# Turning two batches' exponentials through DRAM instead of on TensorE, and moving a clamp from VectorE to ScalarE

## The chip, the cores and the metric

The kernel runs on one core of one Trainium2 chip. The metric is the device time of one launch in microseconds (us), the median of several runs. The engines are named as the profile names them: PE is TensorE (matrix products and transposes through the array), PEld its weight loads, DVE is VectorE, ACT is ScalarE, SP is the engine whose queue issues all DMAs here, POOL is GpSimd.

## The reference

Inputs are `x` (8 batches, 8 heads, 512 positions, 64), `state` (8, 8, 32, 64), `moe_w_in` (512 x 2048) and `moe_w_out` (2048 x 512); all are float32, and the two weights arrive as 64-bit floats (two 32-bit words each). Cut to what matters:

```python
scores  = x @ state.T / 8        # per batch and head: 512 x 32
xread   = softmax(scores) @ state
scores2 = state @ x.T / 8        # 32 x 512
e2      = exp(scores2 - scores2.max(-1))
sread   = (e2 / (e2.sum(-1) + 1e-9)) @ x          # 32 x 64
tokens  = concat([xread, sread], positions)       # (8*544) x 512
h       = tokens @ w_in                           # (8*544) x 2048
out     = (h * sigmoid(1.702*h)) @ w_out          # (8*544) x 512
```

## The kernel before

The order of the instructions on every engine is the order of the program; nothing is rescheduled. Three parts matter.

**The weights.** Each of 32 pieces (16 of w_in, then 16 of w_out: one piece is 128 rows x 512 columns) is loaded as pairs of words and put together as float32. VectorE takes the exponent bits (`mask`), they are clamped to the range of float32 and rescaled (`round_a`), and VectorE makes the number of fraction and exponent (`fraction`, `round_b`). For w_in ScalarE clamps, with two Relu passes; for w_out VectorE clamps, with two passes.

```python
def mask(i):
    _, hi = words(i)
    sc = low[:, 2 + i % (AHEAD + 1)].bitcast(I32)
    power[i] = sc
    nc.vector.tensor_scalar(sc, hi, 0x7FF00000, None, ALU.bitwise_and)        # L207

def round_a(i):
    if i not in power:
        mask(i)
    sc = power[i]
    if PIECES[i][0] == "o":
        nc.vector.tensor_scalar(sc, sc, most, least, ALU.min, ALU.max)        # L215
        nc.vector.tensor_scalar(sc, sc, -least, 8.0, ALU.add, ALU.mult)       # L216
        return
    nc.scalar.activation(out=sc.bitcast(FP32), in_=sc, func=AF.Relu, bias=edge[0], scale=-8.0)    # L218
    nc.scalar.activation(out=sc, in_=sc.bitcast(FP32), func=AF.Relu, bias=edge[1], scale=-1.0)    # L219

def round_b(i, ahead, follows):
    if i not in begun:
        fraction(i)                                                           # L225
    ...                    # dst: the piece's place; lo, hi: its words; sc: its exponent
    nc.vector.scalar_tensor_tensor(sc, hi, -0x80000000, sc, ALU.bitwise_and, ALU.bitwise_or)      # L236
    powers_to(ahead)       # mask and round_a of the pieces up to `ahead`
    nc.vector.scalar_tensor_tensor(dst, lo, 2.0**-32, dst.bitcast(I32), ALU.mult, ALU.add)        # L239
    if follows and i + 1 in raw:
        fraction(i + 1)
    nc.vector.scalar_tensor_tensor(dst, dst, 2.0**-20, sc.bitcast(FP32), ALU.mult, ALU.mult)      # L243

def round_to(n, ahead=AHEAD):
    ...
        powers_to(i + 1)
        round_b(i, min(i + 1 + ahead, max(nin, i + 1)), i + 1 < nin and (i + 1 < n or i >= NPR))
    # nin = 16: the number of w_in's pieces; afterwards the next loads are issued
```

The raw words of w_out's pieces share four places in the tile `later`: piece 4 of w_out can be loaded when piece 0's words have been read (L239), and so on.

**The exponentials.** `sread` multiplies e2, turned so that the 512 positions lie on partitions, with x. For batches 0 and 1 TensorE turned it, and VectorE had multiplied it by the inverse sums; batches 2 to 7 went by 32x32 blocks through DRAM and were scaled after the product.

```python
def s_norm(b, g):
    e, sm = A[b]["e2"][g]
    nc.vector.tensor_scalar(sm, sm, eps, None, ALU.add)
    nc.vector.reciprocal(out=sm, in_=sm)
    if b < 2:
        nc.vector.tensor_scalar(e, e, sm, None, ALU.mult)                     # L381

def eT_out(b):                       # batches 2 to 7; e in 32x32 blocks to DRAM
    for j in range(NPR):
        src = e2_room[b][Ns * j : Ns * (j + 1), :NG].rearrange("n g (t a) -> n (g t) a", a=Ns)
        nc.sync.dma_start(squares[:, :, j], src)                              # L468
def eT_in(b):                        # ... and back, the blocks in their turned places
    ...
    for i in range(SCH):
        nc.sync.dma_start(a["eT"][Ns * i : Ns * (i + 1)].rearrange("n g c q -> n (g c) q"), v[i])   # L476
def eT_turn(b, g):                   # ... and each block turned
    t = A[b]["eT"][:, g].rearrange("p c q -> p (c q)")
    nc.vector.transpose(t, t)                                                 # L480

def att_eT(b, g):                    # batches 0 and 1
    ...
    for c in range(SCH):
        nc.tensor.transpose(ps[:, c], a["e2"][g][0][:, P * c : P * (c + 1)], ident)   # L489
    nc.scalar.copy(a["eT"][:, g], ps)                                         # L490
```

**The loop over w_out's pieces.** It multiplies batch 0 (`down`) while batch 1's hidden rows are still being made (`up_x`, whose gelu is ScalarE's). One turn of it is called a stage.

```python
rounds(1)                            # w_out piece 0; piece 1 follows after four up_x of batch 0
...
rest = list(range(2 * nper, NF))     # the last 8 of the 16 up_x of batch 1
for f in range(NF):                  # NF = 16
    rounds(1)                        # finishes piece f + 2, while there is one
    ...
    if f == NF - 1:
        up_x(1, rest.pop(0))
    for r in range(SCH):
        down(0, r, [f], out_x[0, r], r == SCH - 1)        # 4 products, L542
    if f == 0:
        for b in range(2):
            for g in range(NG):
                att_eT(b, g)
    if f == 1:
        att_sread(0); att_sread(1)                        # L500, copied out by ScalarE
        att_M(1, 2, True); att_M(1, 3)                    # L320, copied out by ScalarE
    if f == 2:
        att_srT(0); att_srT(1)
    if f == 2 or f % 2 == 1 and 1 < f < NF - 1:
        up_x(1, rest.pop(0))                              # L524 on TensorE, gelu L527 on ScalarE
    if f == HF:
        load_state(2); load_x_squares(2)
    if f == NF - 2:
        T_of(T1, B12, B11)                                # L1203: sums of w_out for Strassen's products
        ...
# batch 1: strassen_two, whose products P1, P2 and then the low ones (L689) follow at once
```

Of the kernel before, what the change touches and what calls it, by code (L numbers as in the profile page):

```python
# [10 lines left out]
FP32 = mybir.dt.float32  # L11
I32 = mybir.dt.int32
U32 = mybir.dt.uint32
AF = mybir.ActivationFunctionType
ALU = mybir.AluOpType
# [5 lines left out]
def kernel(  # L21
# [30 lines left out]
    nc = tc.nc  # L52

    B, H, S, D = x.shape
    Ns = state.shape[2]
    DM = H * D
    DF = moe_w_in.shape[1]
    P = 128
    NPR = P // Ns
    NG = H // NPR  # L60
    NF = DF // P
    SCH = S // P
# [3 lines left out]
    NB = S // Ns  # L66
    HF, HN = NF // 2, DM // 2
    scale = float(1.0 / np.sqrt(D))
# [12 lines left out]
    apool = ctx.enter_context(tc.tile_pool(name="apool", bufs=1))  # L81
# [3 lines left out]
    dram = ctx.enter_context(tc.tile_pool(name="dram", bufs=1, space=bass.MemoryType.DRAM))  # L85
# [6 lines left out]
    def att_ps(shape, name):  # L92
        return psA.tile(shape, FP32, tag="att", name=name)

    ident = konst.tile([P, P], FP32, name="ident")
# [70 lines left out]
    PIECES = [("i", c, k) for c in range(NFC) for k in range(NPR)] + [("o", f) for f in range(NF)]  # L166
# [26 lines left out]
    for i, v in enumerate((8.0 * most, 8.0 * (most - least))):  # L193
        t = konst.tile([P, 1], FP32, name=f"edge_{i}")
# [7 lines left out]
# [9 lines that stand above are left out]
        if i not in power:  # L211
            mask(i)
        sc = power[i]
        if PIECES[i][0] == "o":
            nc.vector.tensor_scalar(sc, sc, most, least, ALU.min, ALU.max)  # L215
            nc.vector.tensor_scalar(sc, sc, -least, 8.0, ALU.add, ALU.mult)  # L216
            return
        nc.scalar.activation(out=sc.bitcast(FP32), in_=sc, func=AF.Relu, bias=edge[0], scale=-8.0)  # L218
        nc.scalar.activation(out=sc, in_=sc.bitcast(FP32), func=AF.Relu, bias=edge[1], scale=-1.0)  # L219

    def fraction(i):

        key = PIECES[i]
        dst = w_in[key[1]][:, key[2]] if key[0] == "i" else w_out[:, key[1]]
        nc.vector.tensor_scalar(dst.bitcast(I32), words(i)[1], 0xFFFFF, 0x100000, ALU.bitwise_and, ALU.bitwise_or)  # L225
        begun[i] = dst
# [6 lines that stand above are left out]
        dst = begun.pop(i)  # L233
        lo, hi = words(i)
        sc = power.pop(i)
        nc.vector.scalar_tensor_tensor(sc, hi, -0x80000000, sc, ALU.bitwise_and, ALU.bitwise_or)  # L236
        powers_to(ahead)

        nc.vector.scalar_tensor_tensor(dst, lo, 2.0**-32, dst.bitcast(I32), ALU.mult, ALU.add)  # L239
        del raw[i]  # L240
# [3 lines that stand above are left out]
# [19 lines left out]
    def round_to(n, ahead=AHEAD):  # L263

        nin = NFC * NPR
        while done["b"] < min(n, len(PIECES)):
            i = done["b"]
            powers_to(i + 1)
            round_b(i, min(i + 1 + ahead, max(nin, i + 1)), i + 1 < nin and (i + 1 < n or i >= NPR))
            done["b"] += 1  # L270
            while done["b"] > NPR and done["load"] < len(PIECES) and before(done["load"]) < done["b"]:
                load_weights(done["load"] + 1)
# [12 lines left out]
    A = {b: {} for b in range(B)}  # L285
# [76 lines left out]
    e2_room = {}  # L362

    def att_s_exp(b, room=None):
        a = A[b]
        if room is None:
            room = e2_room[b] = apool.tile([P, NPR, S], FP32, tag="xT", name=f"e2_{b}")
        a["e2"] = []
        for g in range(NG):
            e = room[:, g]  # L370
            sm = apool.tile([P, 1], FP32, tag="sm2", name=f"sm2_{b}_{g}", bufs=4)
            nc.scalar.activation(out=e, in_=a["s"][g], func=AF.Exp, bias=a["mx2"][g], scale=scale, accum_out=sm)
            a["e2"].append((e, sm))

    def s_norm(b, g):

        e, sm = A[b]["e2"][g]
        nc.vector.tensor_scalar(sm, sm, eps, None, ALU.add)
        nc.vector.reciprocal(out=sm, in_=sm)
        if b < 2:  # L380
            nc.vector.tensor_scalar(e, e, sm, None, ALU.mult)  # L381

    def att_s_norm(b):
        for g in range(NG):
# [75 lines left out]
            nc.scalar.copy(m[:, g], ps[g])  # L460


    squares = dram.tile([Ns, NG * NB, NPR, Ns], FP32, name="squares")

    def eT_out(b):
        for j in range(NPR):
            src = e2_room[b][Ns * j : Ns * (j + 1), :NG].rearrange("n g (t a) -> n (g t) a", a=Ns)
            nc.sync.dma_start(squares[:, :, j], src)  # L468

    def eT_in(b):  # L470

        a = A[b]
        a["eT"] = apool.tile([P, NG, SCH, P], FP32, tag="eT", name=f"eT_{b}")
        v = squares.rearrange("n (k i) j a -> i n k (j a)", i=SCH)
        for i in range(SCH):
            nc.sync.dma_start(a["eT"][Ns * i : Ns * (i + 1)].rearrange("n g c q -> n (g c) q"), v[i])  # L476

    def eT_turn(b, g):
        t = A[b]["eT"][:, g].rearrange("p c q -> p (c q)")
        nc.vector.transpose(t, t)  # L480

    def att_eT(b, g):

        a = A[b]
        if g == 0:
            a["eT"] = apool.tile([P, NG, SCH, P], FP32, tag="e1" if b else "eT", name=f"eT_{b}")
        ps = att_ps([P, SCH, P], f"eT_{b}_{g}")
        for c in range(SCH):
            nc.tensor.transpose(ps[:, c], a["e2"][g][0][:, P * c : P * (c + 1)], ident)  # L489
        nc.scalar.copy(a["eT"][:, g], ps)  # L490

    def att_sread(b):

        a = A[b]
        ps = att_ps([P, NG, D], f"sr_{b}")
# [3 lines that stand above are left out]
                    st = slice(Ns * j, Ns * (j + 1))  # L499
                    nc.tensor.matmul(  # L500
                        ps[st, g], a["eT"][:, g, c, st], xn[b][:, c, NG * j + g],
                        start=(c == 0), stop=(c == SCH - 1),
                    )
        sr = apool.tile([P, P], FP32, tag="sr", name=f"sr_{b}", bufs=2)
        if b < 2:
            nc.scalar.copy(sr, ps.rearrange("p g d -> p (g d)"))
        else:
            for g in range(NG):
                nc.scalar.activation(out=sr[:, D * g : D * (g + 1)], in_=ps[:, g], func=AF.Copy, scale=a["e2"][g][1])
        A[b]["sr"] = sr  # L510

    def att_srT(b):
# [607 lines left out]
    def rounds(n):  # L1120
        round_to(done["b"] + n)
# [64 lines left out]
    turn(0, 2, (0, 3))  # L1186
    room = apool.tile([P, NPR, S], FP32, tag="xT", name="e2_01")
    att_s_exp(0, room[:, :NG])
    att_s_exp(1, room[:, NG:])
    rounds(1)  # L1190
    att_s_norm(0)
    att_s_norm(1)
# [27 lines left out]
    for f in range(NF):  # L1220
        rounds(1)
        round_to(NFC * NPR + f + 1)
        if f == NF - 1:

            up_x(1, rest.pop(0))
        for r in range(SCH):
            down(0, r, [f], out_x[0, r], r == SCH - 1)
        if f == 0:
            for b in range(2):
                for g in range(NG):  # L1230
                    att_eT(b, g)
        if f == 1:

            att_sread(0)
            att_sread(1)
            att_M(1, 2, True)
            att_M(1, 3)
        if f == 2:
            att_srT(0)
            att_srT(1)  # L1240
        if f == 2 or f % 2 == 1 and 1 < f < NF - 1:
            up_x(1, rest.pop(0))
        if f == HF:
            load_state(2)
            load_x_squares(2)
        if f == NF - 2:
            T_of(T1, B12, B11)
            low_away(6, B22)
            low_made(5, T1, 1)
            for u in range(NU - 1):  # L1250
                s12(1, u, S)
            T_of(T2, B22, T1)
            low_third(T1)
            for u in range(NU - 1):
                s3(1, u, S)
            T_of(B12, B22, B12)
            low_away(3, T3)
            low_third(T3)
        if f == NF - 1:
            turn_x(2)  # L1260
            low_made(2, T2, 0)
# [6 lines left out]
    for b in range(1, B):  # L1268
        if b > 1:
            ahead = {"P1a": [(up_strassen(b, S, *parts_x(b), A[b]["sums"]), ())]}  # L1270
        else:
            ahead = {
                "P1a": [(low_third, (B22,)), (T_of, (T4, B21, T2)), (low_third, (T2,)), (low_away, (4, T4)), (low_third, (T4,))]
            }
# [19 lines left out]
        k = 3 if b + 1 < B else 0  # L1294
# [40 lines left out]
```

## Time and profile before

| what | before |
|---|---|
| time, median of 3 runs | 708.99 us (708.97 to 709.4) |
| span of the profiled run | 706.9 us |
| VectorE busy | 602.4 us (85%) |
| ScalarE busy | 230.8 us (33%) |
| L489, 16 transposes of e on TensorE | 2.2 us busy, 81.3 to 83.7 us |
| L215 and L216 | 0.43 us each |
| L218 and L219, the same clamp on ScalarE | 0.71 and 0.72 us each |
| L480, the turn of 128x512 on VectorE | 0.69 us each |

How to read the profile: its page gives the busy time of each engine, the chain of work that ended last (followed back from the last instruction, at each step to what released it), and groups of instructions by line of the kernel, with tile names `out<-in`. A view in order of time has a start, a length, the engine, the line, and in brackets the idle time before it and what ended that. [...] neighbours overlap: the difference of two starts is what an instruction costs in a full row. One 128x512 product is listed as two instructions (x2).

### The profile page before, as it was taken

Reading aid. Unit: us, or ns where it says so; the run is one execution under the profiler, and the core shown is the slowest. Engines: PE = TensorE matmul, PEld = TensorE weight load, DVE = VectorE, ACT = ScalarE, POOL = GpSimd, SP = SyncE. Lnnn points to the kernel's source line nnn. Section 1 sums busy time; section 2 is a strip of 40 time slices with the busy share of each in tenths; the row PEclk is TensorE's granted clock in tenths of the full one; section 3 lists DMA queues with packets and bytes.
Section 4 is the critical chain, followed back from the end, with each engine's and each line's share of the span. In section 5 each row is a group of like instructions: output and inputs, shape, how many; then the busy total and the mean of one; then the engine's idle time right before and its main releaser. Section 6 shows DMA issues by size and latency. Waiting matters only on the chain.

```text
span 706.9 us, 12667 instructions
## 1 busy us (share of the span) xinstructions
PE 694.9 (98%) x4973; PEld 558.1 (79%) x4975; DVE 602.4 (85%) x1246; ACT 230.8 (33%) x456; POOL 0.8 (0%) x8
## 2 busy tenths in 40 slices
PE   8989999999999999999999999999999999999996
PEld 3433544458998799879988899889987998899995
DVE  6999799999978998799978996899789987888650
ACT  5686520014224413433243423342243124200210
POOL 0000000000000000000000000000000000000000
PEclk9999999999999999999999999999999999999999
DMA  8921246228742384309550765047432940041001
GB/s 230 368 74 54 93 146 154 115 89 206 213 118 37 61 194 145 69 9 206 148 105 1 152 182 120 16 82 199 137 51 48 194 148 16 0 125 57 16 1 29
DMA packets 143914, 77.89 MB, mean 110 GB/s; under 512 B 113904, under 2 KB 127728, under 8 KB 143856
## 3 DMA queue, kind: packets, MB, share of 16 engines
q1 hardware_dynamic: 143856, 77.09, 42.3%
q8 instruction: 39, 0.64, 0.4%
q14 instruction: 19, 0.16, 0.1%
HBM read 61.08 MB, written 15.99 MB: 109 GB/s over the span
## 4 chain that ended last, share of the span: by engine, by line
PE 95%; ACT 2%; DMA 2%; SPq 0%; DVE 0%; issue 0%; DVEq 0%
PE low L689 21%; PE o L1051 17%; PE o L738 14%; PE o L689 10%; PE o L542 8%; PE h L524 7%; PE upx L1051 6%; PE M L320 4%; PE o L585 2%; PE o L320 1%; PE sr L500 1%; PE warm L125 1%; PE upx_sr L1051 1%; DMA out_dram<-osb_sr 1%; DMA xn<-in_x_dram 1%; ACT low L219 1%
## 5 line engine op out<-in xcount | busy, mean ns | idle before, releaser
L1061 DVE TENSOR_TENSOR g<-o,g 128x512 f32<-128x512 f32 (+1 forms) x140 | 88.0, 650 | 51.1 <-PE o L1051 50.1
L738 PE MATMUL o<-w_out,g 128*128 128x256 f32 x448 | 100.6, 381 | 0.0
L738 PEld LDWEIGHTS o<-w_out,g 128*128 128x128 f32 x448 | 84.4, 190 | 16.6 <-issue 5.5
L1058 ACT ACTIVATE g<-g 128x512 f32<-128x512 f32 (+1 forms) x84 | 49.8, 600 | 100.9 <-DVE g L1061 100.9
L1051 PE MATMUL upx<-aT,M 128*128 128x256 f32 x192 | 49.3, 379 | 0.0
L1051 PE MATMUL o<-ta,M 128*128 128x256 f32 x192 | 49.3, 379 | 0.0
L1051 PE MATMUL o<-ta,ms 128*128 128x256 f32 x192 | 48.3, 379 | 0.0
L689 PE MATMUL low<-low,g 128*128 128x128 f32 x336 | 44.4, 275 | 0.0
L689 PEld LDWEIGHTS low<-low,g 128*128 128x128 f32 x336 | 40.9, 192 | 0.0
L460 ACT COPY M<-M 128x512 f32<-128x512 f32 x64 | 33.1, 598 | 22.7 <-PE M L320 22.7
L1051 PEld LDWEIGHTS o<-ta,ms 128*128 128x128 f32 x192 | 36.6, 190 | 4.9
L1051 PEld LDWEIGHTS o<-ta,M 128*128 128x128 f32 x192 | 36.6, 190 | 4.9
L1051 PEld LDWEIGHTS upx<-aT,M 128*128 128x128 f32 x192 | 36.1, 191 | 4.6
L689 PE MATMUL low<-sums,later 128*128 128x128 f32 x280 | 37.0, 275 | 0.0
L689 PEld LDWEIGHTS low<-sums,later 128*128 128x128 f32 x280 | 34.6, 192 | 0.4
L320 PE MATMUL M<-w_in,stT 64*32 64x512 f32 x512 | 31.9, 594 | 0.0
L527 ACT ACTIVATE g<-h 128x512 f32<-128x512 f32 x24 | 14.0, 591 | 54.7 <-PE h L524 54.7
L524 PE MATMUL h<-low,M 128*128 128x512 f32 x64 | 29.6, 597 | 1.5 <-DVE low L408 1.5
L524 PE MATMUL h<-aT,M 128*128 128x512 f32 x64 | 28.7, 599 | 1.4 <-ACT M L460 1.4
L689 PE MATMUL low<-w_out,g 128*128 128x128 f32 x224 | 29.6, 275 | 0.0
L542 PE MATMUL o<-w_out,g 128*128 128x512 f32 x64 | 28.6, 594 | 0.0
L542 PE MATMUL o<-w_out,sums 128*128 128x512 f32 x64 | 28.3, 593 | 0.0
(210 smaller groups left out, 1295.2 us busy)
## 6 DMA issues: line engine op xcount, KB each, us to landing
low<-low SPq DMA_DIRECT2D x78, 256.0 KB, 3.8
later<-in_moe_w_out_dram SPq DMA_DIRECT2D x16, 512.0 KB, 3.6
xn<-in_x_dram SPq DMA_DIRECT2D x28, 256.0 KB, 4.8
low<-low SPq DMA_DIRECT2D x9, 768.0 KB, 4.0
w_out<-in_moe_w_in_dram SPq DMA_DIRECT2D x12, 512.0 KB
xsq<-in_x_dram SPq DMA_DIRECT2D x96, 64.0 KB, 2.3
out_dram<-osb SPq DMA_DIRECT2D x18, 256.0 KB, 3.1
out_dram<-later SPq DMA_DIRECT2D x14, 256.0 KB, 2.2
```

What stands on the lines that cost most here:

```text
L125: nc.tensor.matmul(ps, zeros[:, :P], zeros, start=True, stop=True)
L320: nc.tensor.matmul(ps[g][st], A[b]["stT"][rows, st], rhs(rows, j), start=True, stop=True)
L460: nc.scalar.copy(m[:, g], ps[g])
L524: nc.tensor.matmul(hps, lhs[i], rhs[i], start=(i == 0), stop=(i == n - 1))
L527: nc.scalar.activation(out=G[key, f // 2][:, f % 2, :ntok], in_=hps, func=AF.Gelu_apprx_sigmoid)
L542: nc.tensor.matmul(ops, G[key, f // 2][:, f % 2, P * r : P * (r + 1)], w_out[:, f], start=(f == 0), stop=(f == NF - 1))
L585: nc.tensor.matmul(ps[:, r], lhs[f][:, P * r : P * (r + 1)], rhs[:, f], start=(first and r == 0 and f == 0), stop=(f == HF - 1), skip_grou ...
L689: nc.tensor.matmul(ps, lhs[f], rhs[:, f], start=(first and f == 0), stop=(f == QF - 1), skip_group_check=True)
L738: nc.tensor.matmul(ps[:, r], lhs[f][:, P * r : P * (r + 1)], rhs[:, f], start=(r == 0 and f == 0), stop=(f == HF - 1), skip_group_check=True,)
L1051: nc.tensor.matmul(ps[:, k], lhs[i][:, o : o + P], rhs[i], start=(first and k == 0 and i == 0), stop=(i == n - 1), skip_group_check=True,)
L1058: nc.scalar.activation(out=dst, in_=src, func=AF.Gelu_apprx_sigmoid)
L1061: nc.vector.tensor_tensor(out=dst, in0=ps, in1=x, op=ALU.add)
```

## The change

The exponentials of batches 0 and 1 go the way of the other batches: out to DRAM by 32x32 blocks right after the exp, back in stage 1, turned by VectorE in stage 4. TensorE no longer transposes them, and the inverse sums are applied when `sread` is copied out. `sread` and what hangs on it moves from stages 1 and 2 to stages 5 and 6, and the eight `up_x` from stages 2, 3, 5, 7, 9, 11, 13 and 15 to stages 6 to 12 and 15.

For w_out's pieces 2 to 15 ScalarE clamps the exponents in the two Relu passes that w_in has, and `mask` and these passes are issued one piece ahead, so that they can run while VectorE puts the piece before together. The aim is to take the transposes from TensorE and the clamps from VectorE.

```diff
@@ round_a
-        if PIECES[i][0] == "o":
+        if PIECES[i][0] == "o" and PIECES[i][1] < 2:
             nc.vector.tensor_scalar(sc, sc, most, least, ALU.min, ALU.max)
             nc.vector.tensor_scalar(sc, sc, -least, 8.0, ALU.add, ALU.mult)
             return
@@ round_to
-            round_b(i, min(i + 1 + ahead, max(nin, i + 1)), i + 1 < nin and (i + 1 < n or i >= NPR))
+            last = min(i + 1 + ahead, nin) if i < nin else i + 2
+            round_b(i, last, i + 1 != nin and (i + 1 < n or i >= NPR))
@@ s_norm
-        if b < 2:
-            nc.vector.tensor_scalar(e, e, sm, None, ALU.mult)
@@ eT_out, eT_in: squares is now one of two DRAM tensors, squares[b % 2]
-    def att_eT(b, g):
-        ... (cut: removed whole)
@@ att_sread
-        if b < 2:
-            nc.scalar.copy(sr, ps.rearrange("p g d -> p (g d)"))
-        else:
-            for g in range(NG):
-                nc.scalar.activation(out=sr[:, D * g : D * (g + 1)], in_=ps[:, g], func=AF.Copy, scale=a["e2"][g][1])
+        for g in range(NG):
+            nc.scalar.activation(out=sr[:, D * g : D * (g + 1)], in_=ps[:, g], func=AF.Copy, scale=a["e2"][g][1])
@@ before the loop
     att_s_exp(0, room[:, :NG])
     att_s_exp(1, room[:, NG:])
+    eT_out(0)
+    eT_out(1)
     rounds(1)
@@ in the loop
-        if f == 0:
+        if f == 1:
+            eT_in(0)
+            eT_in(1)
+        if f == 4:
             for b in range(2):
                 for g in range(NG):
-                    att_eT(b, g)
-        if f == 1:
+                    eT_turn(b, g)
+        if f == 5:
             att_sread(0)
             att_sread(1)
             att_M(1, 2, True)
             att_M(1, 3)
-        if f == 2:
+        if f == 6:
             att_srT(0)
             att_srT(1)
-        if f == 2 or f % 2 == 1 and 1 < f < NF - 1:
+        if 5 < f < NF - 3:
             up_x(1, rest.pop(0))
```

More of the change, by code (lines that the diff above doesn't have):

```diff
@@ L366, in att_s_exp @@
         if room is None:
-            room = e2_room[b] = apool.tile([P, NPR, S], FP32, tag="xT", name=f"e2_{b}")
+            room = apool.tile([P, NPR, S], FP32, tag="xT", name=f"e2_{b}")[:, :NG]
+        e2_room[b] = room
         a["e2"] = []
@@ L460, in att_M @@
             nc.scalar.copy(m[:, g], ps[g])
-    squares = dram.tile([Ns, NG * NB, NPR, Ns], FP32, name="squares")
+    squares = [dram.tile([Ns, NG * NB, NPR, Ns], FP32, name=f"squares_{i}") for i in range(2)]
     def eT_out(b):
         for j in range(NPR):
-            src = e2_room[b][Ns * j : Ns * (j + 1), :NG].rearrange("n g (t a) -> n (g t) a", a=Ns)
-            nc.sync.dma_start(squares[:, :, j], src)
+            src = e2_room[b][Ns * j : Ns * (j + 1)].rearrange("n g (t a) -> n (g t) a", a=Ns)
+            nc.sync.dma_start(squares[b % 2][:, :, j], src)
     def eT_in(b):
         a = A[b]
-        a["eT"] = apool.tile([P, NG, SCH, P], FP32, tag="eT", name=f"eT_{b}")
-        v = squares.rearrange("n (k i) j a -> i n k (j a)", i=SCH)
+        a["eT"] = apool.tile([P, NG, SCH, P], FP32, tag="e1" if b == 1 else "eT", name=f"eT_{b}")
+        v = squares[b % 2].rearrange("n (k i) j a -> i n k (j a)", i=SCH)
         for i in range(SCH):
@@ L480, in eT_turn @@
         nc.vector.transpose(t, t)
-    def att_eT(b, g):
[L484 to L490, printed above, removed]
     def att_sread(b):
```

## The prediction

> **What bounds the kernel now.** I read the page first, then the time-ordered views of TensorE, VectorE and ScalarE over the stretch that the change touches (60 to 200 us). From the page:
>
> ```profile
> span 706.9 us, 12667 instructions
> PE 694.9 (98%) x4973; PEld 558.1 (79%) x4975; DVE 602.4 (85%) x1246; ACT 230.8 (33%) x456; POOL 0.8 (0%) x8
> PE 95%; ACT 2%; DMA 2%; SPq 0%; DVE 0%; issue 0%; DVEq 0%
> ```
>
> TensorE is 98% busy and carries 95% of the chain that ended last: the kernel ends when TensorE has done its list, so what counts is TensorE work removed and TensorE waits added. TensorE in order of time (start, length, what):
>
> ```profile
> 77.83 3.60 PE L542 MATMUL o<-w_out,g 128*128 128x512 f32 x8
> 81.26 1.03 PE L489 MATMUL eT<-ident,e 128*128 128x128 f32 x8
> 82.53 1.15 PE L489 MATMUL eT<-ident,e 128*128 128x128 f32 x8 [0.24 <-ACT eT L490]
> 83.52 3.60 PE L542 MATMUL o<-w_out,g 128*128 128x512 f32 x8
> ...
> 134.09 1.88 PE L524 MATMUL h<-low,M 128*128 128x512 f32 x4
> ...
> 172.51 1.06 PE L689 MATMUL o<-low,spare_M 128*128 128x128 f32 x8
> ...
> 180.55 1.11 PE L689 MATMUL low<-sums,g 128*128 128x128 f32 x8
> ```
>
> Records overlap, so I go by starts: four `down` products of one piece take 3.43 us (77.83 to 81.26), one `up_x` 1.72 us. VectorE in the same form:
>
> ```profile
> 77.47 0.43 DVE L215 TENSOR_SCALAR low<-low 128x512 int32<-128x512 int32 x1
> 77.93 0.43 DVE L216 TENSOR_SCALAR low<-low 128x512 int32<-128x512 int32 x1
> ...
> 127.97 0.68 DVE L236 SCALAR_TENSOR_TENSOR low<-later,low 128x512 int32<-128x512 int32 x1
> ...
> 129.90 2.28 DVE L1203 TENSOR_TENSOR sums<-w_out 128x2048 f32<-128x2048 f32 x1
> ...
> 170.83 0.68 DVE L745 TENSOR_TENSOR osb<-o,g 128x512 f32<-128x512 f32 x1
> ...
> 180.22 0.23 DVE L694 TENSOR_TENSOR later<-low,pu 128x128 f32<-128x128 f32 x1
> ```
>
> The last w_out piece is finished at 129.9, some 20 us before TensorE multiplies by it, but VectorE does not rest there: it goes straight on to the Strassen sums, and from 129.90 to past 180 no wait stands before any of its instructions. The table of stages says the same for 129.9 to 172:
>
> ```profile
> 129.90:172.00 42.10, 42.10 (x188) 25.32 (x187) 41.34 (x58) 10.37 (x20) 0.00 (x0) 1.00 0.45 144
> ```
>
> The columns are length, then busy time of PE, PEld, DVE, ACT, POOL: DVE 41.34 of 42.10. Both engines are full here, and VectorE leads by little: it frees bank 1 (`osb<-o`) at 171.5 and TensorE writes that bank at 172.51; the sum at 180.22 ends at about 180.4 and TensorE's next product starts at 180.55. So VectorE's early finish of the pieces is not spare. ScalarE:
>
> ```profile
> 90.15 2.05 ACT L460 COPY M<-M 128x512 f32<-128x512 f32 x4 [0.78 <-PE M L320]
> ...
> 127.42 0.60 ACT L527 ACTIVATE g<-h 128x512 f32<-128x512 f32 x1 [7.99 <-PE h L524]
> 136.01 0.60 ACT L527 ACTIVATE g<-h 128x512 f32<-128x512 f32 x1 [7.99 <-PE h L524]
> ```
>
> It is mostly idle, but its idle time is spent at the head of its queue, waiting for TensorE's `up_x` (7.99 us before one gelu).
>
> [...] nothing overtakes a gelu that waits. [...] for batches 2 to 7 such a turn of 128x512 takes 0.69 us here. [...] 128 KB of `squares<-e` in 128-byte runs lands 4.5 us after issue, 512 KB of w_out 3.6 us.
>
> **The change, part by part.**
> (1) TensorE loses 16 transposes of e with one wait: 81.26 to 83.52, minus 2.26 us on the path. This is the only gain on the path.
> (2) VectorE loses four multiplications of e (0.49 each, 2 us) and the two clamping passes of 14 pieces, 0.80 us a piece by starts (77.47 to 78.27), 11 us; it gains four turns, 4 x 0.6 = 2.4 us. None of this is on the path by itself.
> (3) ScalarE gains 28 passes. The same two passes for w_in take 0.71 and 0.72 us, about 1.45 us a piece. 14 x 1.45 = 20 us on an engine 33% busy.
> (4) The passes enter ScalarE's queue in program order. From f = 6 to 12 every stage now has one `up_x`, and the passes of piece f+3 are queued in stage f, behind the gelu of stage f-1. So they wait for TensorE. The last, piece 15, sits behind the gelu of `up_x(1, 13)` in stage 11.
>
> When is that? TensorE's new list, without waits: f0 at 77.83, six `down` groups back to back, 77.83 + 6 x 3.43 = 98.41; then sread and two M, 3.80 (87.05 to 90.85 before): f6 at 102.21. Stage 6 with srT is 5.48 (90.85 to 96.33), the rest 5.14 each (96.33 to 101.47): f12 starts at 102.21 + 5.48 + 5 x 5.14 = 133.4. (Before, `up_x(1, 13)` ended at 135.8: the order is new, the amount is the old one less 2.26.) The gelu starts 0.2 after it (136.01 against 135.81), and the next instruction 0.49 later: 134.1. Two passes: 135.6. VectorE then has three instructions left of piece 15, 1.93 us (127.97 to 129.90): 137.5. Only then can it begin the sum that it began at 129.90. **VectorE enters its full stretch 7.6 us later**, though it has 11 us less to do, because it spends about 2.6 of each 5.14 us stage waiting.
>
> From there its list is the old one without a gap to absorb anything. Bank 1 is freed at 171.5 + 7.6 = 179.1, and TensorE, 2.26 us early, would want it at 170.25: it stalls. ScalarE's exp in front of the copy of the first low product is late by the same amount, as it waits for VectorE's maxima. The smallest lead in the stretch is about 0.1 us (180.4 against 180.55), so TensorE comes out 7.6 - 0.1 to 0.2 = 7.4 us later than before; the 2.26 us are swallowed by this stall. After about 200 us VectorE has gaps again (its first wait, 0.97 us, is at 200.23) but TensorE is then full to the end and cannot catch up.
> (5) Small waits before stage 6. The load of piece 4 is now issued behind eight squares DMAs (0.7 us or more each from about 74.6, so at 81), lands at 85 to 86, and its mask stands in VectorE's queue before piece 3 is finished: that is then at about 87.5 to 88.3, needed at 88.12. And in stage 5 ScalarE has the passes of piece 8 in front of the four sr copies (VectorE's turns end near 98, mask of piece 8 at 99.2, passes to 100.7, copies to 101.9), while the second M, at about 101.3, wants their banks: 0.6 us. Together I take 0.6 us; it delays stage 11 and so counts in full.
> Sum: 709.0 + 7.4 + 0.6 = 717.0 us, 1.1% slower.
>
> **The rivals.**
> A: VectorE's lead is slack. Then only (1) counts: 709.0 - 2.3 = 706.7. For it: TensorE 98% busy, 95% of the chain, no wait on VectorE on the page after 60 us. Against it: 41.34 of 42.10 us and leads of 0.1 to 1 us. A chain of waits shows only what ended last; it shows no near miss.
> B: the squares come late. Two batches write and read 4 x 128 KB each way, among the weights. If the turns end 3 us later than I place them, sread waits for that long, and stage 11 with it: 719 to 720. For it: the 4.5 us landing and the single queue. Against it: the turns are four stages after the writes, the reads issue near 88 to 93 and land near 97.
> C: the stall is partly eaten, if VectorE's work in the stretch has hidden waits of under 0.1 us each that no view prints: with 2 us of these, 715.
> I hold the main line at some 75%, A at 8%, B at 10%, C at 7%.
>
> **Range and chances.** The arithmetic of (4) rests on measured spacings, so its error is a few tenths; (5) could be 0 to 2 us. 717.0, with 715.2 to 718.9 for 8 in 10. Two per cent is 14.2 us, which none of these reaches: within 2% 0.95; faster 0.01; slower 0.04 (several late loads on top of the stall).
>
> **What would show it.** Right: no L489 rows, TensorE's first six `down` groups back to back; VectorE idle before the `low<-later,low` instruction of pieces 10 to 15, about 2.6 us each, released by ScalarE; the first L1203-type sum (`sums<-w_out`) starting near 137.5 to 138.5; TensorE waiting 6 to 10 us in sum on VectorE and ScalarE in the first low product after P2, then none. Wrong: if that sum starts by 131, the coupling in (4) fails; if it starts at 138 and TensorE shows no wait, the claim of no slack fails; if TensorE waits at sread for the turned exponentials, B has happened.

## The result, and the profile after

| | before | changed |
|---|---|---|
| time, median of 4 runs | 708.98 us (708.92 to 709.4) | 718.6 us (718.28 to 720.06) |
| ratio, 95% interval | | 1.0138 (1.0121 to 1.0156) |
| VectorE busy | 602.4 us | 590.9 us |
| ScalarE busy | 230.8 us | 249.0 us |
| start of the first Strassen sum | 129.90 us | 140.05 us |

The change takes 2.26 us off TensorE's list and 11.5 us of work from VectorE, and the kernel is 9.6 us slower. Lines are counted anew in the changed kernel: L1194 is the old L1203, L219 and L220 are ScalarE's clamp, L513 and L516 `up_x` and its gelu, L531 `down`, L538 and L539 the copies and stores of batch 0's outputs, L323 the M products, L492 and L498 `sread` and its copies, L727 batch 1's first Strassen products, L678 the low products, L687 ScalarE's copies of them, L683 and L734 VectorE's sums for them. Its page:

```profile
span 716.9 us, 12663 instructions
PE 697.5 (97%) x4959; PEld 558.8 (78%) x4959; DVE 590.9 (82%) x1218; ACT 249.0 (35%) x482; POOL 0.8 (0%) x8
PE 84%; DVE 7%; DMA 4%; ACT 4%; issue 1%; SPq 0%; DVEq 0%
```

TensorE's part of the chain that ended last fell from 95% to 84%, and that of VectorE, ScalarE and DMA rose from 4% to 15%: other engines now decide for some time when TensorE goes on. Where, TensorE's view in order of time shows, with the wait in brackets:

```profile
88.88 10.57 PE L531 MATMUL o<-w_out,g 128*128 128x512 f32 x24 [0.39 <-DVE w_out L244]
...
103.26 1.50 PE L323 MATMUL M<-w_in,stT 64*32 64x512 f32 x16 [0.76 <-ACT sr L498]
...
164.25 6.14 PE L727 MATMUL o<-w_out,g 128*128 128x256 f32 x16 [3.99 <-ACT osb L538]
170.32 1.45 PE L323 MATMUL o<-xsq,stT 64*32 64x512 f32 x16
...
180.77 1.16 PE L678 MATMUL low<-sums,later 128*128 128x128 f32 x8 [1.84 <-ACT pu L687]
...
184.05 1.16 PE L678 MATMUL o<-sums,spare_M 128*128 128x128 f32 x8 [0.28 <-DVE spare_M L683]
...
190.41 1.11 PE L678 MATMUL low<-sums,g 128*128 128x128 f32 x8
```

The last line is the product that started at 180.55 before: TensorE is 9.86 us late there, and keeps about that to the end (the span is 10.0 us longer). The cause stands in two other queues, in the same view. VectorE, then ScalarE:

```profile
138.11 0.69 DVE L237 SCALAR_TENSOR_TENSOR low<-later,low 128x512 int32<-128x512 int32 x1 [2.58 <-ACT low L220]
...
140.05 2.29 DVE L1194 TENSOR_TENSOR sums<-w_out 128x2048 f32<-128x2048 f32 x1
...
190.07 0.23 DVE L683 TENSOR_TENSOR later<-low,pu 128x128 f32<-128x128 f32 x1
```

```profile
136.12 0.60 ACT L516 ACTIVATE g<-h 128x512 f32<-128x512 f32 x1 [3.19 <-PE h L513]
...
137.36 0.72 ACT L220 ACTIVATE low<-low,edge 128x512 int32<-128x512 f32 x1
```

Read from below: ScalarE waits 3.19 us for TensorE's `up_x`, does the gelu, and only then the two passes for piece 15, which need nothing of that gelu (VectorE's mask for them had started at 133.57 and took 0.42 us). VectorE waits 2.58 us for them, finishes the piece and starts the sums at 140.05, 10.15 us later than before. The sum at 190.07 is the one that stood at 180.22: after 50 us of full work VectorE is still 9.85 us late, so this stretch made up for 0.3 us and no more.

### The profile page after: what moved, and what is told of

Read it like the earlier page. It is cut to its first block, busy times and chain, and to the rows that moved or that the text cites. A ratio compares the mean times of both kernels' runs of the same rounds, so it can differ in the third digit from the quotient of the medians.

```text
span 716.9 us, 12663 instructions
## 1 busy us (share of the span) xinstructions
PE 697.5 (97%) x4959; PEld 558.8 (78%) x4959; DVE 590.9 (82%) x1218; ACT 249.0 (35%) x482; POOL 0.8 (0%) x8
## 4 chain that ended last, share of the span: by engine, by line
PE 84%; DVE 7%; DMA 4%; ACT 4%; issue 1%; SPq 0%; DVEq 0%
PE low L678 20%; PE o L1040 17%; PE o L727 12%; PE o L678 10%; PE upx L1040 6%; PE h L513 5%; PE M L323 4%; PE o L531 3%; PE o L574 2%; DMA later<-in_moe_w_out_dram 2%; PE o L323 1%; PE warm L125 1%; DVE sums L1194 1%; PE upx_sr L1040 1%; DMA out_dram<-osb_sr 1%; PE sr L492 1%
## 5 line engine op out<-in xcount | busy, mean ns | idle before, releaser
L727 PE MATMUL o<-w_out,g 128*128 128x256 f32 x448 | 103.2, 387 | 4.0 <-ACT osb L538 4.0
L727 PEld LDWEIGHTS o<-w_out,g 128*128 128x128 f32 x448 | 85.8, 194 | 21.9 <-issue 5.5
L678 PE MATMUL low<-low,g 128*128 128x128 f32 x336 | 44.4, 275 | 0.0
L678 PEld LDWEIGHTS low<-low,g 128*128 128x128 f32 x336 | 40.9, 192 | 0.0
L678 PE MATMUL low<-sums,later 128*128 128x128 f32 x280 | 37.1, 275 | 1.8 <-ACT pu L687 1.8
L678 PEld LDWEIGHTS low<-sums,later 128*128 128x128 f32 x280 | 34.6, 192 | 2.4 <-ACT pu L687 2.0
L323 PE MATMUL M<-w_in,stT 64*32 64x512 f32 x512 | 32.9, 594 | 0.8 <-ACT sr L498 0.8
L513 PE MATMUL h<-low,M 128*128 128x512 f32 x64 | 29.5, 597 | 1.5 <-DVE low L410 1.5
L513 PE MATMUL h<-aT,M 128*128 128x512 f32 x64 | 28.7, 599 | 1.4 <-ACT M L462 1.4
L237 DVE SCALAR_TENSOR_TENSOR low<-later,low 128x512 int32<-128x512 int32 x20 | 13.8, 688 | 19.3 <-ACT low L220 19.2
L678 PE MATMUL low<-w_out,g 128*128 128x128 f32 x224 | 29.6, 275 | 0.0
L687 ACT COPY pu<-low 128x128 f32<-128x128 f32 x21 | 5.6, 267 | 67.7 <-PE low L678 63.5
L531 PE MATMUL o<-w_out,g 128*128 128x512 f32 x64 | 28.3, 595 | 0.4 <-DVE w_out L244 0.4
```

Source lines behind the costliest of these rows:

```text
L323: nc.tensor.matmul(ps[g][st], A[b]["stT"][rows, st], rhs(rows, j), start=True, stop=True)
L513: nc.tensor.matmul(hps, lhs[i], rhs[i], start=(i == 0), stop=(i == n - 1))
L531: nc.tensor.matmul(ops, G[key, f // 2][:, f % 2, P * r : P * (r + 1)], w_out[:, f], start=(f == 0), stop=(f == NF - 1))
L678: nc.tensor.matmul(ps, lhs[f], rhs[:, f], start=(first and f == 0), stop=(f == QF - 1), skip_group_check=True)
L727: nc.tensor.matmul(ps[:, r], lhs[f][:, P * r : P * (r + 1)], rhs[:, f], start=(r == 0 and f == 0), stop=(f == HF - 1), skip_group_check=True,)
```

## The experiments

All times are medians, beside the kernel before on the same chip (708.84 to 708.98). The table is the main finding; a sum's start is read from VectorE's view in order of time of the profiled run.

| run | first Strassen sum, us after 129.90 | time, us over before |
|---|---|---|
| the change | 10.15 | 9.6 |
| e1 squares only | 1.61 | 2.0 |
| e2 clamp only | 11.26 | 10.9 |
| e3 sum three times | 4.76 (the next instruction: 136.86 against 132.10) | 4.4 |
| e4 two ahead | 7.77 | 7.1 |
| e6 store moved | 10.23 | 10.6 |
| e8 two ahead, later | 4.93 | 5.0 |
| e5 pieces early | -5.13 | -0.4 |
| e7 combined | -5.90 | -0.4 |
| e9 combined, late sread | -1.39 | 4.5 |
| e10 sread first | -5.60 | -2.1 |

Where VectorE is later than before, the time grows by that lateness within 0.7 us. Where it is earlier, TensorE's waits before stage 7 decide.

**e1, squares only.** The clamp of all w_out pieces goes back to VectorE.

```diff
-        if PIECES[i][0] == "o" and PIECES[i][1] < 2:
+        if PIECES[i][0] == "o":
@@ round_to: as in the kernel before
```

> The changed kernel with the clamp given back to VectorE (two passes a piece, none ahead); squares, turns and the new places of sread and up_x stay. Main theory (ScalarE's passes, queued behind the gelus, make VectorE late): VectorE no longer waits for ScalarE in the loop; 3.5 us a piece and a turn of 2.5 to 4 us put the first Strassen sum at about 132 to 133 instead of 129.9 (before) or 140.05 (changed), and the end 2 to 3 us after the kernel before: 710.5 to 712. Rival (the squares' DMAs among the weights are what costs): the loss stays, 717 or more. Rival (VectorE's lead is slack): 707 to 708.

Measured 710.8 us, ratio 1.0029 (1.0017 to 1.0041). VectorE, in order of time:

```profile
131.51 2.28 DVE L1193 TENSOR_TENSOR sums<-w_out 128x2048 f32<-128x2048 f32 x1
```

The squares alone cost little: VectorE has the four turns more and is 1.6 us late, and the 2.26 us taken from TensorE do not show. The rival of slack (707 to 708) falls, and so does the one that puts the loss on the squares' DMAs.

**e2, clamp only.** The kernel before with both edits of e1 the other way round: clamp on ScalarE, one piece ahead, nothing else.

> The kernel before with the clamp of pieces 2 to 15 on ScalarE, one piece ahead; TensorE still transposes, all else is as before. Main theory: the passes of piece 15 lie behind the gelu of the up_x in stage 11, which ends at 136.0 before, so the first Strassen sum starts at 139.5 to 141 and the time is 718 to 720, as much lost as with the whole change, though no squares are written. Rival (squares cost it): 709 or less, as VectorE has 11 us less work.

Measured 719.77 us, ratio 1.0154 (1.0139 to 1.0169): all of the loss, without a square of batches 0 and 1 written. (The line numbers are the old ones, one or two higher in part.) ScalarE in order of time:

```profile
137.23 0.60 ACT L528 ACTIVATE g<-h 128x512 f32<-128x512 f32 x1 [4.05 <-PE h L525]
...
138.47 0.72 ACT L219 ACTIVATE low<-low,edge 128x512 int32<-128x512 f32 x1
```

It is the gelu of the same `up_x`, at the old place of the loop, and the same order behind it. The clamp on ScalarE alone is thus enough for the loss; that it is the place in the queue, and not the two passes themselves, e8 and e5 will show. The losses of e1 and e2 do not add up to that of the change (2.0 and 10.9 against 9.6): both act on the same start of the sums, and in the changed kernel, as I read it, the turns fall into time in which VectorE would have waited anyway.

**e3, the first sum three times.** Nothing of the change; VectorE is made late by hand.

```diff
+            T_of(T1, B12, B11)
+            T_of(T1, B12, B11)
             T_of(T1, B12, B11)
```

> The kernel before with its first Strassen sum (2.2 us on VectorE by starts) issued three times, which changes no value: VectorE is 4.4 us later in the full stretch and nothing else is touched. Main theory (the lead is 0.1 to 0.2 us): 709.0 + 4.3 = 713.2. Rival (the lead is slack of several us): 709 to 710.

Measured 713.22 us, ratio 1.0063 (1.0046 to 1.0079). In VectorE's view the three sums take 6.86 us from start to start of the next instruction, instead of 2.20:

```profile
130.00 6.94 DVE L1203 TENSOR_TENSOR sums<-w_out 128x2048 f32<-128x2048 f32 x3
136.86 0.68 DVE L1203 TENSOR_TENSOR away<-w_out 128x512 f32<-128x512 f32 x1
...
184.68 0.23 DVE L694 TENSOR_TENSOR later<-low,pu 128x128 f32<-128x128 f32 x1
```

So 4.66 us went in; 4.46 us are left at the sum that stood at 180.22, and the time grew by 4.4: the stretch has some 0.3 us of slack. TensorE first waits 0.79 us at 164.50, behind batch 0's outputs (e6 is about this path), and then in the low products:

```profile
175.38 1.16 PE L689 MATMUL low<-sums,later 128*128 128x128 f32 x8 [1.72 <-ACT pu L698]
```

It waits for ScalarE's copy, which stands behind the exp, which waits for VectorE's maxima:

```profile
173.61 0.69 ACT L372 ACTIVATE e<-o,mx 128x512 f32<-128x512 f32 x1 [0.44 <-DVE mx L359]
```

The same wait for this copy, of 1.84 us, is in the changed kernel.

**e4 and e8, two pieces ahead.** If the place in the queue decides, one stage earlier must gain one stage, 5.15 us.

```diff
-            last = min(i + 1 + ahead, nin) if i < nin else i + 2
+            last = min(i + 1 + ahead, nin) if i < nin else i + 2 + (i >= nin + 7)     # e4; e8: nin + 9
```

> The changed kernel with the mask and ScalarE's passes two pieces ahead instead of one from piece 7 on, so that the passes of piece 15 are queued one stage earlier, behind the gelu of stage 10. One stage is 5.15 us. Main theory: first Strassen sum at 134.9 instead of 140.05, time 5.0 us under the changed kernel: 713.6. Rival (squares, or the load of the weights): no change, 718 to 719.

e4: 715.92 us (713.19 to 716.54), ratio 1.0092 (1.0072 to 1.0111): only 2.7 us gained. TensorE, in order of time:

```profile
104.39 2.05 PE L323 MATMUL M<-w_in,stT 64*32 64x512 f32 x16 [2.32 <-ACT sr L498]
```

The expectation failed because a second pair of passes now stood in front of sread's copies; TensorE waited 2.3 us for them instead of 0.76, its clock fell to 0.5 between 106 and 108 us, and stage 7 began 2.77 us later than in the changed kernel (112.94 against 110.17). 5.15 - 2.77 = 2.4, and the sum started 2.38 us earlier. e8 takes that away:

> As e4, but the second piece ahead begins with piece 9 instead of 7, so that only one pair of passes stands in front of sread's copies, as in the changed kernel. In e4 two pairs stood there, TensorE waited 2.3 us for the copies instead of 0.8, and its clock fell to half for some 3 us after that wait; stage 7 began 2.8 us later than in the changed kernel, and the gain was 2.7 us instead of 5.0. Main theory: with that gone the whole stage is gained: first Strassen sum at 134.9, time 713.3 to 714. Rival (one stage earlier in ScalarE's queue is worth only half a stage for some other reason): 715.5 to 716.5.

e8: 713.88 us, ratio 1.0070 (1.0056 to 1.0085). This is the median of three runs; a fourth, of 903.3 us at a mean granted clock of 0.753, is left out.

```profile
134.83 2.29 DVE L1194 TENSOR_TENSOR sums<-w_out 128x2048 f32<-128x2048 f32 x1
```

The same passes, one stage earlier in the queue, are worth 5.22 us of VectorE's start.

**e6, the store behind the outputs.** The prediction had no wait at 164.25, where TensorE stood 3.99 us. The DMA queue's view of the changed kernel shows where it comes from:

```profile
159.57 0.32 SPq L637 DMA_DIRECT2D low<-away  x1
159.98 10.06 SPq L539 DMA_DIRECT2D out_dram<-osb  x4
```

The first store waits for sums that VectorE, late, finishes only then, and batch 0's outputs, ready from 151 us on, are issued behind it. e6 issues them in front.

```diff
-            low_away(3, T3)
+            room3 = low_away(3, T3, False)        # sums only
@@ after the last stage's down products
+            low_keep(3, room3)
```

> The changed kernel with one DMA moved in the queue: the store of the Strassen parts of the third room is issued behind the four stores of batch 0's last outputs instead of in front of them. In the changed kernel it waits for VectorE until 159.6 and holds the first output's store, so ScalarE's second output copy waits 12.3 us and TensorE 4.0 us at 164.3. Main theory: that wait is covered by VectorE's lateness, which alone sets the end; the 4.0 us wait goes and the time stays at 718 to 719. Rival (the wait and the slow products after it are part of the loss): 4 to 6 us faster, 713 to 715.

Measured 719.48 us, ratio 1.0149 (1.0135 to 1.0163). The wait at 164.25 is gone and nothing is gained; TensorE waits for VectorE's sums, and then for ScalarE's copy behind VectorE's maxima:

```profile
174.78 2.04 PE L678 MATMUL low<-low,spare_M 128*128 128x128 f32 x8 [3.70 <-DVE spare_M L734]
180.84 2.08 PE L678 MATMUL low<-sums,later 128*128 128x128 f32 x8 [4.01 <-ACT pu L687]
```

It is no faster at all: after the pauses, now inside the low products, TensorE stands at half clock until about 184 us (granted 0.78 from 172 to 176 us, 0.50 from 176 to 184, 0.94 from 184 to 188; these products take 2.04 and 2.08 us instead of 1.06), and VectorE waits 0.78 us for one of them in turn.

**e5, two pieces a stage in stages 6 to 9.**

```diff
     for f in range(NF):
-        rounds(1)
+        rounds(2 if 5 < f < 10 else 1)
```

> The changed kernel with two pieces a stage finished in stages 6 to 9 instead of one in 6 to 13; the passes of piece 15 then lie behind the gelu of stage 8 (120.7). Main theory: the first Strassen sum starts near 125, VectorE then waits once for the gelu of stage 11 and enters the full stretch at or ahead of TensorE, so TensorE keeps its 2.26 us less the 2.5 us of waits before stage 6: 708.5 to 709.5. Rival (something other than VectorE's lateness holds TensorE from 156 us on, such as the outputs' DMAs): 713 or more.

Measured 708.47 us, ratio 0.9994 (0.9986 to 1.0002): the whole loss is gone with no work removed, only the order changed.

```profile
124.77 2.28 DVE L1194 TENSOR_TENSOR sums<-w_out 128x2048 f32<-128x2048 f32 x1
```

VectorE starts the sums 5.13 us earlier than before, and TensorE waits for nothing behind stage 6. The 2.26 us are still given back before stage 7, which begins at 110.22 where the sum without waits says 107.69.

**e7 and e9, two attempts on the waits before stage 7.** e7 is e5 with `eT_out` behind piece 0 and the turns in stage 5; e9 also puts sread and the M products into the middle of stage 6, and srT into stage 7.

> The run before last (two pieces a stage in stages 6 to 9) with the squares written behind piece 0's turn, so that the load of piece 4 is issued ahead of them, and VectorE's turns in stage 5 behind piece 7, so that the passes of piece 8 are not queued in front of the copies of sread. Main theory: the waits of about 2.5 us before stage 6 shrink to 0.5 or less and the 2.26 us of the transposes come through: 706.7 to 707.5, faster than the kernel before by 0.2 to 0.3%. Rival (the turned blocks still come late, or VectorE is late again): 708.5 or more.

e7: 708.45 us (707.41 to 709.41), ratio 0.9993 (0.9985 to 1.0001), against 706.7 to 707.5 expected. The wait for piece 3 is gone, but sread waits 1.1 us. The profile names ScalarE's clamp as the releaser; I put it to VectorE's turns, the first of which started at 98.86 us, just before sread at 99.67, behind a mask whose load was 2.0 us late.

> As e7, but sread and the two M of batch 1 are put between the second and the third product of stage 6, and srT in stage 7. In e7 TensorE waited 1.1 us at sread for VectorE's turns, which stood behind a mask whose load was late by 2.0 us, and stage 7 began at 109.33 where the sum without waits says 107.69. Main theory: the turned blocks are there by then and the copies of M pass under the two remaining products; stage 7 begins at 107.6 to 108.0 and the time is 706.7 to 707.3, below the kernel before by 0.2 to 0.3%. Rival (a later wait, or VectorE's lead, gives it back): 708 to 709.

e9: 713.42 us (709.94 to 714.05), ratio 1.0057 (1.0041 to 1.0074), against 706.7 to 707.3: a miss, by the mechanism under study. Stage 6 now issued two pieces before sread, so three pairs of passes stood in front of sread's copies. ScalarE, then TensorE, in order of time:

```profile
105.31 0.72 ACT L219 ACTIVATE low<-low,edge 128x512 f32<-128x512 int32 x1 [1.09 <-DVE low L207]
...
106.69 0.91 ACT L498 ACTIVATE sr<-sr,sm 128x64 f32<-128x64 f32 x4
```

```profile
107.25 1.79 PE L323 MATMUL M<-w_in,stT 64*32 64x512 f32 x16 [3.63 <-ACT sr L498]
```

**e10, sread first.** e9 with the two pieces of stage 6 issued behind sread and M:

```diff
-        rounds(2 if 5 < f < 10 else 1)
+        if f != 6:
+            rounds(2 if 5 < f < 10 else 1)
@@ in stage 6, after the second down product
                 att_sread(0); att_sread(1); att_M(1, 2, True); att_M(1, 3)
+                rounds(2)
```

> As e9, but stage 6's two pieces are issued behind sread and the M of batch 1 instead of in front of them. In e9 three pairs of passes (pieces 8, 9 and 10) stood in ScalarE's queue in front of sread's copies; TensorE waited 3.6 us for the copies, and the time was 713.4. Main theory (the order in ScalarE's queue is what decides): that wait goes; stage 7 begins at 107.6 to 108.2, the time is 706.6 to 707.4, 0.2 to 0.3% below the kernel before. Rival (the late turns or DMAs hold sread anyway): 708 to 709, as e7.

Measured **706.75 us** (706.57 to 707.39), ratio 0.9971 (0.9960 to 0.9983): faster than both kernels, 2.13 us under the kernel before, of the 2.26 us that the transposes took. Its page and TensorE's view:

```profile
PE 95%; ACT 2%; DMA 2%; SPq 0%; DVE 0%; issue 0%; DVEq 0%
```

```profile
100.25 1.10 PE L492 MATMUL sr<-xn,eT 128*32 128x64 f32 x64
...
104.18 1.98 PE L531 MATMUL o<-w_out,g 128*128 128x512 f32 x4
...
107.71 3.60 PE L531 MATMUL o<-w_out,g 128*128 128x512 f32 x8
```

No bracket is left here, and none on TensorE from 60 us to the end; stage 7 begins at 107.71, and TensorE carries 95% of the chain again.

## Why the prediction was right

**The mechanism (4).** Right. VectorE waits 2.58 us in each of pieces 11 to 15, as put at 2.6. e2 shows the clamp alone makes the loss; e5 and e8 show that it is the place in the queue and not the work. It holds for the passes of pieces 10 to 15; those before stood behind no gelu that waited for TensorE.

**No slack in VectorE's stretch.** Right to 0.3 us, and shown by itself in e3: 4.66 us in, 4.4 us out. Rival A falls with it. So does rival C, which had put 2 us into hidden waits of VectorE: 10.15 us of lateness went into the stretch and 9.85 came out. The place that bound was not the sum at 180.22 that I had picked for its small lead: TensorE's last wait is the 0.28 us at 184.05, and at 185.05 as at 190.41 it is 9.86 us late.

**The size.** 717.0 was predicted, 718.6 measured; the sum was to start at 138.1 with the small waits, and started at 140.05. The term that was too small is (5): I took 0.6 us for the waits before stage 6, and stage 6 began at 104.69 instead of 102.21, 2.5 us late. Of this 0.2 us is an offset present from stage 0, 0.6 us the wait for piece 3 (the load of piece 4 was held up as described, and VectorE waited 2.75 us for it before it finished piece 3), 0.3 us sread, which began 0.2 us late and ran 0.1 us longer, and 1.4 us the two M, the second behind sread's copies: a wait of 0.76 us, after which its 16 listed instructions took 1.43 us by starts, where half of the 32 of both M took 0.94 before. VectorE's turns waited 1.3 us for the squares on their way back, so a little of rival B was in it. The 4.5 us to landing that I had for the squares was the median of writing and reading batch 2's together; the 24 writes in the kernel before have a median of 3.0 us, so these figures do not show that 128 KB in short runs land later than 512 KB (3.6 us). In the changed kernel the writes took 3.4 us and the way back 5.8. With 2.5 in place of 0.6 the sum gives 709.0 + 7.4 + 2.5 = 718.9.

**Where TensorE would wait.** Partly wrong. I had placed all of its waiting in the first low product, 6 to 10 us. There it waited 2.1 us; 4 us stood earlier, at batch 0's output, and about 2.5 us were slow products after that, at a granted clock of 0.50 (the next group came 6.78 us late, against 4.26 before it). I had not followed VectorE's lateness through the DMA queue. That the number held all the same is no merit of this part: as e6 shows, VectorE's lateness came through (719.48 against 718.6 us) with this wait or without it.

**What (1) was worth.** The 2.26 us were indeed swallowed; e10 brings 2.13 of them back.

## What to carry to other kernels

Where work moves to an idle engine, ask what stands in front of it in that engine's queue, not how busy the engine is. ScalarE was 33% busy, but the passes of the last six pieces stood behind a gelu that waited for TensorE (1.39 us in front of piece 10's passes, 3.19 us in front of each of the five after), and in e4 and e9 the same passes held up the copies behind them (TensorE waited 2.32 and 3.63 us). And VectorE, which had finished the weights some 20 us early, had no slack, as what came next was full (41.34 of 42.10 us busy): follow such an engine's list until it first waits, here at 200 us, before counting its lead as spare.

## What was not expected of the hardware

TensorE's pause at batch 0's output cost more than its length. The table of stages of the changed kernel (length, busy PE, PEld, DVE, ACT, POOL, then the granted clock):

```profile
164.00:168.00 4.00, 3.75 (x9) 3.03 (x10) 3.96 (x6) 0.79 (x2) 0.00 (x0) 0.50 0.22 82
```

Behind the 3.99 us wait the granted clock is 0.50 for this whole stage (0.79 in the 4 us before it, 0.85 in the 4 us after it; 1.00 from 164 to 168 us in the kernel before), and 16 products that took 3.62 us before it take 6.14. In e4's profiled run a listed wait of 2.32 us was followed by 0.50 as well (106 to 108 us), and in e9's one of 3.63 us by 0.58 and 0.57 (108 to 110 and 110 to 112 us). The 1.84 us wait in the changed kernel's low product was not: the clock stayed at 1.00 from 176 to 188 us.

The runs of one kernel differ in their mean granted clock. In e4 the run of 713.19 us, near the 713.6 expected, had 1.0, the other three (715.61 to 716.54 us) 0.996 to 0.999; in e9 one run of 709.94 us had 0.999 and the other five (712.8 to 714.05 us) 0.994 to 0.996. From these numbers I would guess that in the two short runs the clock did not fall; no trace of them was kept, so this is not shown.
